# Softmax row sums: a ones-matmul with Ln and Exp against a transposing reduction, a 16-column matmul and a transpose

## The chip, the cores and the metric

One core of one Trainium2 chip runs the whole program in one launch. The metric is the time of one execution on the device, in microseconds (us), as the median of several executions. All the runs used here are of the undisturbed ("fast") kind; the executions of one kernel lie mostly within 0.4% of each other. The experiments were timed in several rounds and on several chips, where the kernel before took between 367.5 and 368.2 us (medians), so a difference between runs of different rounds is uncertain by about 0.6 us. In this text PE is TensorE's matmul stream, PEld its weight loads, DVE is VectorE, ACT is ScalarE, POOL is GpSimd, SP is the engine that issues most DMAs.

## The reference

Two independent attention blocks, A and B, with grouped heads, each followed by an output projection; the two results stand side by side.

```python
# B=16, Sq=32, D=1024, Hq=32 query heads, Hkv=4 key/value heads, Sk=512, Dh=128, all bf16
q = (x @ wq).reshape(B, Sq, Hq, Dh).transpose(0, 2, 1, 3)
k, v = repeat(k_cache, 8, axis=1), repeat(v_cache, 8, axis=1)
p = softmax(einsum("bhqd,bhkd->bhqk", q, k) * Dh ** -0.5, axis=-1)
o = einsum("bhqk,bhkd->bhqd", p, v)
out = o.transpose(0, 2, 1, 3).reshape(B, Sq, Hq * Dh) @ wo
```

## The kernel before

The work is cut into 128 slots, one for each (problem, batch, key/value head). A slot has 8 heads x 32 queries = 256 columns (QW) and 512 keys in KC = 4 chunks of P = 128 partitions. In the code SQ = 32 is the queries of a slot, REP = 8 its heads, and NG = 64 the pairs of slots. Scores are computed transposed (keys on partitions), ScalarE takes the exponential with a fixed shift in place of a maximum, and the values matmul leaves its result with head dimension on partitions and query columns along the free axis. The softmax denominator of a column is therefore a sum over *partitions*, and it is wanted on all 128 partitions, to scale a [128, 256] block. Before, two adds on VectorE sum the four chunks, and a matmul with a matrix of ones sums over partitions and broadcasts at once; Ln and Exp(-x) on ScalarE make the reciprocal.

```python
def partial_sums(i):                       # each slot, VectorE
    t1 = work.tile([P, 2, QW], FP32, name="t1", bufs=1)
    nc.vector.tensor_tensor(out=t1[:], in0=p_sb[:, 0:2, :], in1=p_sb[:, 2:4, :], op=ALU.add)
    ...
    nc.vector.tensor_tensor(out=tsum[j][:, q, :], in0=t1[:, 0, :], in1=t1[:, 1, :], op=ALU.add)

def pair_sums(j):                          # each pair of slots
    sums = psum.tile([P, 2, QW], FP32, name="sums", tag="sums", bufs=1)
    nc.tensor.matmul(sums[...], lhsT=ones[:], rhs=tsum.pop(j)[...], start=True, stop=True)  # 512 columns
    nc.scalar.activation(out=lg[:], in_=sums[:], func=ACTF.Ln)
    nc.scalar.activation(out=rcp[j][:], in_=lg[:], func=ACTF.Exp, scale=-1.0)
    nc.gpsimd.dma_start(out=lall[j:j + 1, :], in_=lg[0:1, ...])   # for a range check at the end
```

`normalize` multiplies `rcp` into `ob`, the PSUM result of the values matmuls; `ob` has one buffer for a pair of slots, so the next pair's values wait for it. TensorE's remaining work, the projections of q and of the output, is cut into single 512-column matmuls ("units"), and about 6.75 of them are strewn into every slot so that TensorE always has something to do:

```python
for i in range(total_slots + 2):
    j, odd = divmod(i - 2, 2)               # live: slot i exists; j >= 0: a pair two slots back
    if live: do_loads(i); scores(i)
    if odd and j >= 0: normalize(2 * j)
    run(units, 3)
    if not odd and j >= 0: pair_sums(j)
    run(units, 1 if odd else 3)
    if j >= 0: values(2 * j + odd)          # two slots behind
    if live: partial_sums(i)
    run(units, 3 - (i % 4 == 3) if odd else 1)
    if odd and j >= 0: normalize(2 * j + 1)
```

Keys and values come by DMA four slots at a time, from a pool `kv` with two buffers each for `kT` and `v_sb`. These loads, and all but the first of the weights', stand in SP's queue in program order.

Of the kernel before, what the change touches and what calls it, by code (L numbers as in the profile page):

```python
# [8 lines left out]
BF16 = mybir.dt.bfloat16  # L9
FP32 = mybir.dt.float32  # L10
FP32R = mybir.dt.float32r
I32 = mybir.dt.int32
ACTF = mybir.ActivationFunctionType
ALU = mybir.AluOpType
AX = mybir.AxisListType

P = 128
HQ = 32
DH = 128
HKV = 4  # L20
REP = HQ // HKV
HALF = REP // 2
SCALE = float(DH) ** -0.5

SHIFT = 44.0
ONES = 2.0 ** -75
LIMIT = 20.0


def general_path(tc, problems, out_flat):  # L30
# [142 lines left out]
def kernel(  # L173
# [35 lines left out]
    def fast_path(ok_i):  # L209
        with ExitStack() as fctx:  # L210
            enter = fctx.enter_context
            const = enter(tc.tile_pool(name="const", bufs=1))
            blk = enter(tc.tile_pool(name="blk", bufs=20))
            kv = enter(tc.tile_pool(name="kv", bufs=2))
            work = enter(tc.tile_pool(name="work", bufs=2))
            outp = enter(tc.tile_pool(name="outp", bufs=3))
            psum = enter(tc.tile_pool(name="psum", bufs=2, space=bass.MemoryType.PSUM))
# [11 lines left out]
            nc.vector.memset(warm[:], 0.0)  # L229
            ident = const.tile([P, P], BF16, name="ident")  # L230
            make_identity(nc, ident[:])
            ones_f = const.tile([P, P], FP32, name="ones_f")
            nc.vector.memset(ones_f[:], ONES)
            ones = const.tile([P, P], FP32R, name="ones")
            nc.vector.tensor_copy(out=ones[:], in_=ones_f[:])
            one_col = const.tile([P, 1], FP32, name="one_col")
            nc.vector.memset(one_col[:], 1.0)
            shift = const.tile([P, 1], FP32, name="shift")
            nc.vector.memset(shift[:], SHIFT)
            cnt = const.tile([P, 1], FP32, name="cnt")  # L240
            nc.vector.memset(cnt[:], 0.0)
            NLR = NG
            lall = const.tile([NLR, 2 * QW], FP32, name="lall")


            def blk_tile(shape, name, dtype=BF16):
                return blk.tile(shape, dtype, name=name, tag="blk")
# [54 lines left out]
            def q_units(pr, h):  # L302
                g, hl = divmod(h, REP)
                if hl == 0:
                    qT[pr, g] = blk_tile([P, B, REP, SQ], "qT")
                w = wq_tiles[pr, h // 4]
                ps = psum.tile([P, NW], FP32, name="q_ps", tag="proj")
                for dc in range(DC):
                    nc.tensor.matmul(  # L309
                        ps[:],  # L310
                        lhsT=w[:, dc, (h % 4) * DH:(h % 4 + 1) * DH],
                        rhs=xT[pr][:, dc, :],
                        start=(dc == 0),
                        stop=(dc == DC - 1),
                    )
                    if dc == DC - 1:
                        nc.vector.tensor_copy(  # L317
                            out=qT[pr, g][:, :, hl, :],
                            in_=ps[:].rearrange("p (b s) -> p b s", s=SQ),
                        )  # L320
                    yield
# [26 lines left out]
            def run(units, n):  # L348
                for _ in range(n):
                    next(units, None)  # L350


            def where(i):
                pr, ii = divmod(i, NG)
                if pr == 0:
                    g, b = divmod(ii, B)
                else:
                    b, g = divmod(ii, HKV)
                return pr, b, g
# [3 lines left out]
            def scores(i):  # L363
                pr, b, g = where(i)
                kT = k_tiles[i // GRP].rearrange("p q (k c) -> p q c k", c=KC)
                s_ps = psum.tile([P, KC, QW], FP32, name="s_ps", tag="s")
                for c in range(KC):
                    nc.tensor.matmul(  # L368
                        s_ps[:, c, :],
                        lhsT=kT[:, i % GRP, c, :],  # L370
                        rhs=qT[pr, g][:, b, :, :].rearrange("p h s -> p (h s)"),
                        start=True,
                        stop=True,
                    )
                p_sb = work.tile([P, KC, QW], BF16, name="p_sb", bufs=4)
                nc.scalar.activation(  # L376
                    out=p_sb[:], in_=s_ps[:], func=ACTF.Exp, bias=shift[:], scale=SCALE
                )
                st[i] = {"p": p_sb}

            tsum, rcp = {}, {}

            def partial_sums(i):
                p_sb = st[i]["p"]
                t1 = work.tile([P, 2, QW], FP32, name="t1", bufs=1)
                nc.vector.tensor_tensor(  # L386
                    out=t1[:], in0=p_sb[:, 0:2, :], in1=p_sb[:, 2:4, :], op=ALU.add
                )
                j, q = divmod(i, 2)
                if q == 0:  # L390
                    tsum[j] = work.tile([P, 2, QW], FP32R, name="t")
                nc.vector.tensor_tensor(
                    out=tsum[j][:, q, :], in0=t1[:, 0, :], in1=t1[:, 1, :], op=ALU.add
                )

            pair = {}

            def pair_sums(j):
                sums = psum.tile([P, 2, QW], FP32, name="sums", tag="sums", bufs=1)
                nc.tensor.matmul(  # L400
                    sums[:].rearrange("p q n -> p (q n)"),
                    lhsT=ones[:],
                    rhs=tsum.pop(j)[:].rearrange("p q n -> p (q n)"),
                    start=True,
                    stop=True,
                )
                lg = work.tile([P, 2, QW], FP32, name="lg")
                nc.scalar.activation(out=lg[:], in_=sums[:], func=ACTF.Ln)  # L408
                rcp[j] = work.tile([P, 2, QW], FP32, name="r")
                nc.scalar.activation(out=rcp[j][:], in_=lg[:], func=ACTF.Exp, scale=-1.0)  # L410
                nc.gpsimd.dma_start(  # L411
                    out=lall[j:j + 1, :],
                    in_=lg[0:1, :, :].rearrange("p q n -> p (q n)"),
                )

            def values(i):
                v_sb = v_tiles[i // GRP]
                j, q = divmod(i, 2)
                if q == 0:
                    pair[j] = psum.tile([P, 2, QW], FP32, name="ob", tag="ob", bufs=1)  # L420
                for c in range(KC):
                    nc.tensor.matmul(  # L422
                        pair[j][:, q, :],
                        lhsT=v_sb[:, i % GRP, c, :],
                        rhs=st[i]["p"][:, c, :],
                        start=(c == 0),
                        stop=(c == KC - 1),
                    )

            def normalize(i):  # L430
                pr, b, g = where(i)
                normalized.add((pr, b, g))
                st.pop(i)
                j, q = divmod(i, 2)
                tt, bl = divmod(b, BPT)
                if (pr, tt) not in oT:
                    oT[pr, tt] = blk_tile([P, HQ, P], "oT")
                nc.vector.scalar_tensor_tensor(  # L438
                    out=oT[pr, tt][:, g * REP:(g + 1) * REP, bl * SQ:(bl + 1) * SQ],
                    in0=rcp[j][:, q, :].rearrange("p (h s) -> p h s", s=SQ),  # L440
                    scalar=ONES,
                    in1=pair[j][:, q, :].rearrange("p (h s) -> p h s", s=SQ),
                    op0=ALU.mult,
                    op1=ALU.mult,
                )


# [115 lines left out]


            total_slots = 2 * NG
            for i in range(total_slots + 2):
                live = i < total_slots
                j, odd = divmod(i - 2, 2)
                if live:
                    do_loads(i)  # L570
                    scores(i)
                if odd and j >= 0:
                    normalize(2 * j)
                run(units, 3)
                if not odd and j >= 0:
                    pair_sums(j)
                run(units, 1 if odd else 3)
                if j >= 0:
                    values(2 * j + odd)
                if live:  # L580
                    partial_sums(i)
                run(units, 3 - (i % 4 == 3) if odd else 1)
                if odd and j >= 0:
                    normalize(2 * j + 1)


            run(units, 8)
            sq = blk_tile([NLR, 2 * QW], "sq", FP32)
            nc.vector.tensor_tensor(out=sq[:], in0=lall[:], in1=lall[:], op=ALU.mult)
            nc.vector.tensor_scalar(  # L590
                out=sq[:], in0=sq[:], scalar1=LIMIT * LIMIT, scalar2=0.0,
                op0=ALU.is_le, op1=ALU.add, accum_out=cnt[0:NLR, :],
            )
            run(units, 16)
            ok_ps = psum.tile([1, 1], FP32, name="ok_ps", tag="s")
            nc.tensor.matmul(ok_ps[:], lhsT=cnt[:], rhs=one_col[:], start=True, stop=True)
# [3 lines left out]
    flag = ctx.enter_context(tc.tile_pool(name="flag", bufs=1))  # L600
    ok_i = flag.tile([1, 1], I32, name="ok_i")
    fast_path(ok_i)
    total = 2 * NG * QW
    ok = nc.values_load(ok_i[0:1, 0:1], min_val=0, max_val=total,
                        skip_runtime_bounds_check_because="only compared")
    with tc.If(ok < total, preferred_fallthrough_block=True, label="general"):
# [31 lines left out]
```

## Time and profile before

| | before |
|---|---|
| time, median of 3 runs | 368.15 us (367.96 to 368.4) |
| span of the profiled run | 367.2 us |
| PE, DVE, ACT busy | 98%, 66%, 60% |
| clock granted to TensorE | 0.998 |

The first line is from the page's table of busy time, the second from its chain of work that ended last, by engine; the groups below them have, on the right of the bar, the busy time of all and the mean ns of one, then the engine's idle time just before them with what ended it.

```profile
PE 359.0 (98%) x2204; PEld 221.9 (60%) x2204; DVE 243.3 (66%) x478; ACT 218.6 (60%) x262; POOL 40.5 (11%) x85
...
PE 92%; DMA 3%; DVE 2%; issue 1%; ACT 1%; DVEq 0%
...
L438 DVE SCALAR_TENSOR_TENSOR oT<-r,ob 128x256 bf16<-128x256 f32 x128 | 53.2, 416 | 2.6 <-ACT r L410 1.6
L410 ACT ACTIVATE r<-lg 128x512 f32<-128x512 f32 x64 | 40.4, 632 | 2.0
L408 ACT ACTIVATE lg<-sums 128x512 f32<-128x512 f32 x64 | 37.8, 590 | 1.8 <-PE sums L400 1.8
L400 PE MATMUL sums<-t,ones 128*128 128x512 f32 x64 | 35.9, 561 | 0.1
...
L400 PEld LDWEIGHTS sums<-t,ones 128*128 128x128 f32 x64 | 12.1, 188 | 9.8 <-issue 2.8
```

TensorE is the limit: busy 98% at full clock, and 92% of the chain. But the 561 ns of one `sums` matmul is not what it takes from TensorE's stream, because the records of matmuls overlap: a 512-column projection matmul has a record of 380 ns, and the next one starts 216 ns after it. What counts is the distance between starts. The next lines are the timeline of PE alone (start, duration, what, how many):

```profile
67.94 0.81 PE L309 MATMUL q_ps<-xT,wq_sb 128*128 128x512 bf16 x3
68.40 0.58 PE L400 MATMUL sums<-t,ones 128*128 128x512 f32 x1
68.83 0.82 PE L309 MATMUL q_ps<-xT,wq_sb 128*128 128x512 bf16 x3
69.48 0.60 PE L422 MATMUL ob<-p_sb,v_sb 128*128 128x256 bf16 x4
```

From 67.94 to 68.83 are 0.89 us, of which three projection matmuls take 3 x 0.216. The `sums` matmul takes the remaining 0.24 us. The one after it comes 11 ns late, so 0.25 us in all, and 64 of them make 16 us. This is the prize.

The rest that can be won on TensorE is waits, of two kinds. From the view of waits (who waited for whom: us, times, longest):

```profile
PEld L422 <- issue: 3.9, 10, 0.5
PE s_ps L368 <- DMA kT<-in_B_k_cache_dram: 1.5, 1, 1.5
PE ob L422 <- DVE oT L438: 1.1, 5, 0.2
```

```profile
30.18 1.03 PE L309 MATMUL q_ps<-xT,wq_sb 128*128 128x512 bf16 x4
...
30.96 0.41 DVE L438 SCALAR_TENSOR_TENSOR oT<-r,ob 128x256 bf16<-128x256 f32 x1
31.43 0.60 PE L422 MATMUL ob<-p_sb,v_sb 128*128 128x256 bf16 x4 [0.22 <-DVE oT L438]
```

One wait is for keys (`kT`), once. The other is for `ob`: values want the buffer before VectorE's normalisation has left it. The view puts 1.1 us on it. (By start distance the one wait for keys is 1.65 us, where the view has 1.5.)

### The profile page before, as it was taken

The page shows a single profiled execution, that of the slowest core. Times are in us where ns is not written, and L with a number is a line of the kernel's source. Part 1 is how long each engine was busy: PE and PEld are TensorE (multiplying, and loading weights), DVE is VectorE, ACT ScalarE, POOL GpSimd, SP SyncE. Part 2 cuts the span into 40 slices and gives each one's busy share as a digit, 9 for nine tenths or more (in the row PEclk, how much of TensorE's full clock was granted, in tenths as well). Part 3 has the DMA queues.
Part 4 walks back from the last instruction along what each step waited for, and adds up shares of the span by engine and source line. Part 5 has one row for each costly group of instructions (what it writes and reads, how often), then busy time and mean ns, then how long its engine had stood idle before and what let it go on. Part 6 is the DMA issues. An engine that isn't in the chain of part 4 may idle for free.

```text
span 367.2 us, 6071 instructions
## 1 busy us (share of the span) xinstructions
PE 359.0 (98%) x2204; PEld 221.9 (60%) x2204; DVE 243.3 (66%) x478; ACT 218.6 (60%) x262; POOL 40.5 (11%) x85
## 2 busy tenths in 40 slices
PE   8999999999999999999999999998999999999995
PEld 5555656666665666666666666665665666666554
DVE  1448787877878777887776667664666666666410
ACT  2127666667666667666666776665766666766200
POOL 0001101111110111110111111111111111111110
PEclk9999999999999999999999999999999999999999
DMA  8998479899797479799999354997447994440000
GB/s 266 310 267 245 105 218 222 194 306 225 209 207 200 96 217 220 221 308 294 322 289 271 97 123 131 253 346 177 131 129 245 339 227 112 113 116 15 17 14 33
DMA packets 127136, 71.86 MB, mean 196 GB/s; under 512 B 75680, under 2 KB 126112, under 8 KB 127104
## 3 DMA queue, kind: packets, MB, share of 16 engines
q1 hardware_dynamic: 122848, 68.24, 69.8%
q0 software_dynamic: 2768, 2.10, 2.1%
q10 hardware_dynamic: 1488, 1.11, 1.0%
q8 instruction: 18, 0.29, 0.3%
q14 instruction: 14, 0.11, 0.1%
HBM read 51.38 MB, written 2.10 MB: 146 GB/s over the span
## 4 chain that ended last, share of the span: by engine, by line
PE 92%; DMA 3%; DVE 2%; issue 1%; ACT 1%; DVEq 0%
PE f_ps L328 28%; PE q_ps L309 28%; PE ob L422 14%; PE s_ps L368 14%; PE sums L400 4%; DMA kT<-in_B_k_cache_dram 3%; PE warm_ps L471 1%; PE q_ps L494 1%; PE xT_ps L480 1%; DVE oT L438 1%; ACT r L410 0%; ACT lg L408 0%; DVE t_544 L386 0%; DVE t_3211 L386 0%; DVE t_1516 L386 0%
## 5 line engine op out<-in xcount | busy, mean ns | idle before, releaser
L376 ACT ACTIVATE p_sb<-s_ps,shift 128x1024 bf16<-128x1024 f32 x128 | 142.7, 1114 | 114.9 <-PE s_ps L368 109.3
L328 PE MATMUL f_ps<-wo_sb,oT 128*128 128x512 bf16 (+1 forms) x544 | 137.0, 367 | 0.0
L309 PE MATMUL q_ps<-xT,wq_sb 128*128 128x512 bf16 x496 | 134.0, 380 | 0.0
L368 PE MATMUL s_ps<-qT,kT 128*128 128x256 bf16 x512 | 76.8, 273 | 1.5 <-DMA kT<-in_B_k_cache_dram 1.5
L422 PE MATMUL ob<-p_sb,v_sb 128*128 128x256 bf16 x512 | 76.8, 272 | 1.1 <-DVE oT L438 1.1
L422 PEld LDWEIGHTS <-v_sb 128*128 128x128 bf16 x512 | 50.1, 98 | 35.8 <-issue 3.9
L368 PEld LDWEIGHTS <-kT 128*128 128x128 bf16 x512 | 56.7, 113 | 23.4 <-DMA kT<-in_B_k_cache_dram 2.0
L328 PEld LDWEIGHTS <-oT 128*128 128x128 bf16 x544 | 50.6, 98 | 33.3 <-issue 7.6
L309 PEld LDWEIGHTS <-wq_sb 128*128 128x128 bf16 x496 | 46.0, 98 | 33.2 <-issue 6.7
L411 POOL DMA_DIRECT2D lall<-lg x64 | 31.3, 489 | 276.1 <-ACT lg L408 276.0
L317 DVE CAST qT<-q_ps 128x512 bf16<-128x512 f32 x62 | 42.8, 690 | 26.1 <-PE q_ps L309 25.3
L438 DVE SCALAR_TENSOR_TENSOR oT<-r,ob 128x256 bf16<-128x256 f32 x128 | 53.2, 416 | 2.6 <-ACT r L410 1.6
L410 ACT ACTIVATE r<-lg 128x512 f32<-128x512 f32 x64 | 40.4, 632 | 2.0
L408 ACT ACTIVATE lg<-sums 128x512 f32<-128x512 f32 x64 | 37.8, 590 | 1.8 <-PE sums L400 1.8
L400 PE MATMUL sums<-t,ones 128*128 128x512 f32 x64 | 35.9, 561 | 0.1
L340 DVE CAST o_sb<-f_ps 128x512 bf16<-128x512 f32 (+1 forms) x16 | 10.8, 674 | 14.9 <-PE f_ps L328 14.7
L400 PEld LDWEIGHTS sums<-t,ones 128*128 128x128 f32 x64 | 12.1, 188 | 9.8 <-issue 2.8
L342 POOL DMA_DIRECT2D out_dram<-o_sb x15 | 8.5, 568 | 40.4 <-DVE o_sb L340 40.1
L338 ACT CAST o_sb<-f_ps 128x256 bf16<-128x256 f32 x1 | 0.4, 372 | 19.1 <-PE f_ps L328 19.1
L484 DVE COPY xT<-xT_ps 128x512 bf16<-128x512 bf16 x4 | 1.7, 425 | 6.4 <-PE xT_ps L480 6.4
L485 ACT COPY xT<-xT_ps 128x512 bf16<-128x512 bf16 x4 | 2.2, 588 | 6.1 <-DVE xT L484 6.1
L471 PE MATMUL warm_ps<-warm 128*128 128x512 bf16 x10 | 4.5, 615 | 1.3 <-DVE warm L229 1.3
(281 smaller groups left out, 162.9 us busy)
## 6 DMA issues: line engine op xcount, KB each, us to landing
v_sb<-in_A_v_cache_dram SPq DMA_DIRECT2D x16, 512.0 KB, 4.8
wq_sb<-in_B_wq_dram SPq DMA_DIRECT2D x8, 1024.0 KB, 6.1
wo_sb<-in_A_wo_dram SPq DMA_DIRECT2D x8, 1024.0 KB, 7.2
v_sb<-in_B_v_cache_dram SPq DMA_DIRECT2D x16, 512.0 KB, 3.9
wo_sb<-in_B_wo_dram SPq DMA_DIRECT2D x8, 1024.0 KB, 8.6
wq_sb<-in_A_wq_dram SPq DMA_DIRECT2D x7, 1024.0 KB, 7.6
out_dram<-o_sb POOLq DMA_DIRECT2D x15, 128.0 KB, 2.3
kT<-in_A_k_cache_dram SPq DMA_TRANSPOSE x64, 3.3
```

The source lines that it names most:

```text
L309: nc.tensor.matmul(ps[:], lhsT=w[:, dc, (h % 4) * DH:(h % 4 + 1) * DH], rhs=xT[pr][:, dc, :], start=(dc == 0), stop=(dc == DC - 1),)
L317: nc.vector.tensor_copy(out=qT[pr, g][:, :, hl, :], in_=ps[:].rearrange("p (b s) -> p b s", s=SQ),)
L328: nc.tensor.matmul(ps[:, 0:width], lhsT=oT[pr, tt][:, h, :], rhs=wo_tiles[pr, nh, h // REP][:, h % REP, off:off + width], start=(h == 0), ...
L340: nc.vector.tensor_copy(out=o_sb[:, 0:width], in_=ps[:, 0:width])
L368: nc.tensor.matmul(s_ps[:, c, :], lhsT=kT[:, i % GRP, c, :], rhs=qT[pr, g][:, b, :, :].rearrange("p h s -> p (h s)"), start=True, stop=True,)
L376: nc.scalar.activation(out=p_sb[:], in_=s_ps[:], func=ACTF.Exp, bias=shift[:], scale=SCALE)
L400: nc.tensor.matmul(sums[:].rearrange("p q n -> p (q n)"), lhsT=ones[:], rhs=tsum.pop(j)[:].rearrange("p q n -> p (q n)"), start=True, stop ...
L408: nc.scalar.activation(out=lg[:], in_=sums[:], func=ACTF.Ln)
L410: nc.scalar.activation(out=rcp[j][:], in_=lg[:], func=ACTF.Exp, scale=-1.0)
L411: nc.gpsimd.dma_start(out=lall[j:j + 1, :], in_=lg[0:1, :, :].rearrange("p q n -> p (q n)"),)
L422: nc.tensor.matmul(pair[j][:, q, :], lhsT=v_sb[:, i % GRP, c, :], rhs=st[i]["p"][:, c, :], start=(c == 0), stop=(c == KC - 1),)
L438: nc.vector.scalar_tensor_tensor(out=oT[pr, tt][:, g * REP:(g + 1) * REP, bl * SQ:(bl + 1) * SQ], in0=rcp[j][:, q, :].rearrange("p (h s) - ...
```

## The change

The intent: TensorE's 512-column matmul becomes one of 16 columns, and Ln and Exp leave ScalarE. VectorE's `tensor_reduce` with `apply_transpose` transposes 32x32 blocks and sums over what was the partition axis, so 32 partitions (a quadrant) are summed in one instruction; the four quadrants are then added by a tiny matmul with a matrix of four by four identities; the reciprocal is taken on 16 columns, and a VectorE transpose of a broadcast view spreads it over 512 columns. To balance the engines, the qT copies move from VectorE to ScalarE. Values run three slots behind in place of two, the kv pool gets a third buffer, and `p_sb`, which waits longer for its values now, five buffers in place of four.

```diff
-            kv = enter(tc.tile_pool(name="kv", bufs=2))
+            kv = enter(tc.tile_pool(name="kv", bufs=3))
...
-                        nc.vector.tensor_copy(
+                        nc.scalar.copy(
                             out=qT[pr, g][:, :, hl, :],
...
-                p_sb = work.tile([P, KC, QW], BF16, name="p_sb", bufs=4)
+                p_sb = work.tile([P, KC, QW], BF16, name="p_sb", bufs=5)
...
-                nc.vector.tensor_tensor(out=t1[:], in0=p_sb[:, 0:2, :], ...)      # and the second add
+                nc.vector.tensor_reduce(
+                    out=parts[j][:, q, :, :].rearrange("p c h -> p (c h)"),
+                    in_=st[i]["p"][:].rearrange("p c (h s) -> p (c h) s", s=SQ),
+                    axis=AX.X, op=ALU.add, apply_transpose=True,
+                )
+            def chunk_sums(j):                       # 128x64 -> 128x16, over the four chunks
+                nc.vector.tensor_reduce(out=cs[:], in_=parts.pop(j)[...], axis=AX.X, op=ALU.add)
+            def fold_sums(j):
+                nc.tensor.matmul(sums[:], lhsT=fold[...], rhs=cs[...], start=True, stop=True)   # 16 columns
+            def reciprocals(j):
+                nc.vector.reciprocal(out=rall[:, j, :], in_=pair.pop(j)[:])
+                nc.vector.transpose(out=r[...], in_=rall[:, j, :].unsqueeze(2).to_broadcast([P, 2 * REP, SQ]))
...                                                   # normalize: one 512-column instruction per pair, not two of 256
-            for i in range(total_slots + 2):
+            for i in range(total_slots + 3):
...
+                run(units, 1)
+                if not odd and 1 <= j <= NG: chunk_sums(j - 1)
+                if i >= 3: values(i - 3)
+                if odd and 1 <= j <= NG: reciprocals(j - 1)
+                if not odd and j >= 2: normalize(j - 2)
+                run(units, 5)
+                if not odd and 1 <= j <= NG: fold_sums(j - 1)
+                if live: partial_sums(i)
+                run(units, 1 - (i % 4 == 3))
```

The 64 small `lall` DMAs go too; the range check now reads the reciprocals, which stay in memory.

More of the change, by code (lines that the diff above doesn't have):

```diff
@@ L21 @@
 REP = HQ // HKV
+QD = 32
 HALF = REP // 2
@@ L25 @@
 SHIFT = 44.0
-ONES = 2.0 ** -75
-LIMIT = 20.0
+SUM_LO = 2.0 ** 46
+SUM_HI = 2.0 ** 104
 def general_path(tc, problems, out_flat):
@@ L231, in fast_path @@
             make_identity(nc, ident[:])
-            ones_f = const.tile([P, P], FP32, name="ones_f")
-            nc.vector.memset(ones_f[:], ONES)
-            ones = const.tile([P, P], FP32R, name="ones")
-            nc.vector.tensor_copy(out=ones[:], in_=ones_f[:])
+            fold = const.tile([P, P // QD, QD], FP32R, name="fold")
+            for r in range(P // QD):
+                rs = slice(r * QD, (r + 1) * QD)
+                nc.vector.tensor_copy(
+                    out=fold[rs],
+                    in_=ident[rs, rs].unsqueeze(1).to_broadcast([QD, P // QD, QD]),
+                )
             one_col = const.tile([P, 1], FP32, name="one_col")
@@ L241, in fast_path @@
             nc.vector.memset(cnt[:], 0.0)
-            NLR = NG
-            lall = const.tile([NLR, 2 * QW], FP32, name="lall")
+            rall = const.tile([P, NG, 2 * REP], FP32, name="rall")
             def blk_tile(shape, name, dtype=BF16):
@@ L379, in scores @@
                 st[i] = {"p": p_sb}
-            tsum, rcp = {}, {}
+            parts, rcp, pair = {}, {}, {}
             def partial_sums(i):
-                p_sb = st[i]["p"]
-                t1 = work.tile([P, 2, QW], FP32, name="t1", bufs=1)
-                nc.vector.tensor_tensor(
-                    out=t1[:], in0=p_sb[:, 0:2, :], in1=p_sb[:, 2:4, :], op=ALU.add
-                )
                 j, q = divmod(i, 2)
                 if q == 0:
-                    tsum[j] = work.tile([P, 2, QW], FP32R, name="t")
-                nc.vector.tensor_tensor(
-                    out=tsum[j][:, q, :], in0=t1[:, 0, :], in1=t1[:, 1, :], op=ALU.add
-                )
-            pair = {}
-            def pair_sums(j):
-                sums = psum.tile([P, 2, QW], FP32, name="sums", tag="sums", bufs=1)
+                    parts[j] = work.tile([P, 2, KC, REP], FP32, name="parts")
+                nc.vector.tensor_reduce(
+                    out=parts[j][:, q, :, :].rearrange("p c h -> p (c h)"),
+                    in_=st[i]["p"][:].rearrange("p c (h s) -> p (c h) s", s=SQ),
+                    axis=AX.X, op=ALU.add, apply_transpose=True,
+                )
+            def chunk_sums(j):
+                cs = pair[j] = work.tile([P, 2, REP], FP32R, name="cs")
+                with nc.allow_low_precision(reason="float32r holds the float32 sum"):
+                    nc.vector.tensor_reduce(
+                        out=cs[:], in_=parts.pop(j)[:].rearrange("p q c h -> p q h c"),
+                        axis=AX.X, op=ALU.add,
+                    )
+            def fold_sums(j):
+                cs = pair[j]
+                sums = pair[j] = psum.tile([P, 2 * REP], FP32, name="sums", tag="sums", bufs=1)
                 nc.tensor.matmul(
-                    sums[:].rearrange("p q n -> p (q n)"),
-                    lhsT=ones[:],
-                    rhs=tsum.pop(j)[:].rearrange("p q n -> p (q n)"),
+                    sums[:],
+                    lhsT=fold[:].rearrange("p r s -> p (r s)"),
+                    rhs=cs[:].rearrange("p q h -> p (q h)"),
                     start=True,
@@ L406, in pair_sums @@
                 )
-                lg = work.tile([P, 2, QW], FP32, name="lg")
-                nc.scalar.activation(out=lg[:], in_=sums[:], func=ACTF.Ln)
-                rcp[j] = work.tile([P, 2, QW], FP32, name="r")
-                nc.scalar.activation(out=rcp[j][:], in_=lg[:], func=ACTF.Exp, scale=-1.0)
-                nc.gpsimd.dma_start(
-                    out=lall[j:j + 1, :],
-                    in_=lg[0:1, :, :].rearrange("p q n -> p (q n)"),
+            def reciprocals(j):
+                nc.vector.reciprocal(out=rall[:, j, :], in_=pair.pop(j)[:])
+                r = rcp[j] = work.tile([P, 2 * REP, SQ], FP32, name="r")
+                nc.vector.transpose(
+                    out=r[:].rearrange("p n s -> p (n s)"),
+                    in_=rall[:, j, :].unsqueeze(2).to_broadcast([P, 2 * REP, SQ]),
                 )
+            ob = {}
             def values(i):
@@ L419, in values @@
                 if q == 0:
-                    pair[j] = psum.tile([P, 2, QW], FP32, name="ob", tag="ob", bufs=1)
+                    ob[j] = psum.tile([P, 2, QW], FP32, name="ob", tag="ob", bufs=1)
                 for c in range(KC):
                     nc.tensor.matmul(
-                        pair[j][:, q, :],
+                        ob[j][:, q, :],
                         lhsT=v_sb[:, i % GRP, c, :],
@@ L428, in values, with normalize @@
                     )
-            def normalize(i):
-                pr, b, g = where(i)
-                normalized.add((pr, b, g))
-                st.pop(i)
-                j, q = divmod(i, 2)
+            def normalize(j):
+                for i in (2 * j, 2 * j + 1):
+                    normalized.add(where(i))
+                    st.pop(i)
+                pr, b, g = where(2 * j)
                 tt, bl = divmod(b, BPT)
@@ L437, in normalize @@
                     oT[pr, tt] = blk_tile([P, HQ, P], "oT")
-                nc.vector.scalar_tensor_tensor(
-                    out=oT[pr, tt][:, g * REP:(g + 1) * REP, bl * SQ:(bl + 1) * SQ],
-                    in0=rcp[j][:, q, :].rearrange("p (h s) -> p h s", s=SQ),
-                    scalar=ONES,
-                    in1=pair[j][:, q, :].rearrange("p (h s) -> p h s", s=SQ),
-                    op0=ALU.mult,
-                    op1=ALU.mult,
+                if pr == 0:
+                    out = oT[pr, tt][:, g * REP:(g + 1) * REP, bl * SQ:(bl + 2) * SQ]
+                    out = out.rearrange("p h (q s) -> p q h s", s=SQ)
+                else:
+                    out = oT[pr, tt][:, g * REP:(g + 2) * REP, bl * SQ:(bl + 1) * SQ]
+                    out = out.rearrange("p (q h) s -> p q h s", h=REP)
+                nc.vector.tensor_tensor(
+                    out=out,
+                    in0=rcp.pop(j)[:].rearrange("p (q h) s -> p q h s", h=REP),
+                    in1=ob.pop(j)[:].rearrange("p q (h s) -> p q h s", s=SQ),
+                    op=ALU.mult,
                 )
@@ L565, in fast_path @@
             total_slots = 2 * NG
-            for i in range(total_slots + 2):
+            for i in range(total_slots + 3):
                 live = i < total_slots
-                j, odd = divmod(i - 2, 2)
+                j, odd = divmod(i, 2)
                 if live:
@@ L571, in fast_path @@
                     scores(i)
-                if odd and j >= 0:
-                    normalize(2 * j)
-                run(units, 3)
-                if not odd and j >= 0:
-                    pair_sums(j)
-                run(units, 1 if odd else 3)
-                if j >= 0:
-                    values(2 * j + odd)
+                run(units, 1)
+                if not odd and 1 <= j <= NG:
+                    chunk_sums(j - 1)
+                if i >= 3:
+                    values(i - 3)
+                if odd and 1 <= j <= NG:
+                    reciprocals(j - 1)
+                if not odd and j >= 2:
+                    normalize(j - 2)
+                run(units, 5)
+                if not odd and 1 <= j <= NG:
+                    fold_sums(j - 1)
                 if live:
                     partial_sums(i)
-                run(units, 3 - (i % 4 == 3) if odd else 1)
-                if odd and j >= 0:
-                    normalize(2 * j + 1)
-            run(units, 8)
-            sq = blk_tile([NLR, 2 * QW], "sq", FP32)
-            nc.vector.tensor_tensor(out=sq[:], in0=lall[:], in1=lall[:], op=ALU.mult)
-            nc.vector.tensor_scalar(
-                out=sq[:], in0=sq[:], scalar1=LIMIT * LIMIT, scalar2=0.0,
-                op0=ALU.is_le, op1=ALU.add, accum_out=cnt[0:NLR, :],
-            )
+                run(units, 1 - (i % 4 == 3))
+            sq = blk_tile([QD, NG * 2 * REP], "sq", FP32)
+            cnt2 = const.tile([P, 2], FP32, name="cnt2")
+            nc.vector.memset(cnt2[:], 0.0)
+            for k, (lim, op) in enumerate(((1.0 / SUM_HI, ALU.is_ge), (1.0 / SUM_LO, ALU.is_le))):
+                nc.vector.tensor_scalar(
+                    out=sq[:], in0=rall[0:QD].rearrange("p j n -> p (j n)"),
+                    scalar1=lim, scalar2=0.0, op0=op, op1=ALU.add,
+                    accum_out=cnt2[0:QD, k:k + 1],
+                )
+            nc.vector.tensor_tensor(out=cnt[:], in0=cnt2[:, 0:1], in1=cnt2[:, 1:2], op=ALU.add)
             run(units, 16)
@@ L602 @@
     fast_path(ok_i)
-    total = 2 * NG * QW
+    total = 2 * 2 * NG * QW
     ok = nc.values_load(ok_i[0:1, 0:1], min_val=0, max_val=total,
```

## The prediction

> **What bounds the kernel now.** TensorE. The page's busy table gives PE 98% of 367.2 us, DVE 66%, ACT 60%, POOL 11%; the chain of waits is 92% PE, clock full throughout. In the two-slot steady state (timeline, 60 to 81 us) a pair of slots takes 4.80 or 5.02 us, and matmuls start back to back: 216 ns for 512 columns, 109 ns for 256. PE waits little: 1.5 us once at 250 us for a kT transpose DMA, 1.1 us in five waits of ob for oT (view of waits). DVE and ACT have slack in every stretch, so what the change does for them is worth nothing by itself; only PE's stream counts.
>
> **Removed from PE.** The 128x512 float32r ones-matmul, 64 times. From the matmul before it to the one after it the start-to-start distance is about 455 ns against 216 without it: 239 ns each, plus 11 ns lost at the next matmul, about 15.5 us (the chain gives it 4.2%, 15.4 us). Its 188 ns weight load hides behind the 512-column matmul before it.
>
> **Added on PE.** The same matmul with 16 columns. The weight load should still hide; the streaming shrinks to almost nothing, but the next weight load cannot hide behind it. The nearest thing in the trace is the one-column fp32 pair of ok_ps: 25 ns to its twin, 96 ns to the next bf16 matmul. Estimate: 95 ns each (60 to 150), 6 us. Net gain about 9.4 us (6 to 12).
>
> **VectorE.** Removed per pair of slots: two adds of 695 ns, two of 425, two normalisations of 416, and 1.7 qT copies of 690 in the first half (these go to ACT, where a 512-column PSUM read takes about 0.6 us). Added: two transposing reductions over 1024 elements. The Trainium skill ("VectorE: DVE Perf Modes", the perf-mode tier table) has tensor_reduce at 1x; this trace's 512-element fp32 ops are 690 ns and 256-element ones 425, i.e. about 1.04 ns an element plus 160, so about 1.22 us each (estimate), if transposing costs nothing per element. Plus a 64-element sum (0.22), a 16-element reciprocal (0.3), a 512-element transpose (0.69) and one merged normalisation (0.7). With the overlap seen between independent instructions this is about 4.1 us per pair in the first half and 4.35 with o_sb copies in the second, against about 4.75 of PE. So DVE rises to about 85 to 92% busy and does not take over; the chain reduction, chunk sum, fold, reciprocal, transpose, normalisation has about 1 us of slack before the single ob buffer is wanted again.
>
> **ACT, POOL, DMA.** ACT loses Ln and Exp (78 us), gains 62 copies (about 37 us): down to about 49%. The 64 small lall DMAs go. Three kv buffers let kT loads run ahead; the 1.5 us kT wait should vanish, and probably most of the ob waits.
>
> **Predicted.** 368.15 - 9.4 - 2.3 + 0.8 for new small waits = 357.2 us, 354 to 364. Faster by over 2% (below 360.8): 0.78; within 2%: 0.13; slower: 0.09.
>
> **What would show it.** PE busy still 96% or more of a shorter span; sums group far below 35.9 us, with 250 ns or less added around each fold; DVE 85 to 92%, reductions about 1.2 us; ACT near 50%; no kT or ob wait over 1 us in total.
>
> **What would make it wrong.** The transposing reduction running at half rate (about 2.3 us): then VectorE needs about 6.5 us per pair and the kernel takes about 460 us. Dependent waits on VectorE pushing normalisation past the next use of ob. An exposed weight load around the fold (188 + 100 ns): then the gain all but disappears. Loads running ahead and delaying weights.

## The result

| | before | after |
|---|---|---|
| time, median of 4 runs | 368.05 us (367.26 to 368.4) | 350.57 us (350.22 to 351.09) |
| span of the profiled run | 367.2 us | 349.1 us |
| PE, DVE, ACT, POOL busy | 98, 66, 60, 11% | 98, 81, 51, 3% |

The ratio is 0.9529 (95% interval 0.9507 to 0.9551). A ratio here is the mean time of one kernel's fast runs over that of the other's of the same rounds, so it is not quite the ratio of the medians. A control of the changed kernel in later rounds gave 350.65 us against 368.15. The gain is 17.5 us; 10.9 were predicted, and 350.6 lies outside the range that began at 354.

The same parts of the page of the changed kernel:

```profile
PE 340.7 (98%) x2163; PEld 221.0 (63%) x2204; DVE 283.4 (81%) x421; ACT 179.6 (51%) x196; POOL 8.9 (3%) x21
...
PE 94%; DMA 3%; issue 1%; DVE 1%; ACT 0%; SPq 0%
...
L390 DVE TRANSPOSE_TENSOR_REDUCE parts<-p_sb 128x32 f32<-128x1024 bf16 x128 | 158.2, 1236 | 21.5 <-ACT p_sb L379 20.9
...
L453 DVE TENSOR_TENSOR oT<-r,ob 128x512 bf16<-128x512 f32 x64 | 43.9, 685 | 12.7 <-PE ob L431 9.3
L320 ACT CAST qT<-q_ps 128x512 bf16<-128x512 f32 x62 | 36.1, 583 | 23.7 <-PE q_ps L312 20.8
L418 DVE STREAM_TRANSPOSE r<-rall 128x512 f32<-128x512 f32 x64 | 45.5, 711 | 2.2
L407 PE MATMUL sums<-cs,fold 128*128 128x16 f32 x64 | 22.9, 357 | 0.1
...
L407 PEld LDWEIGHTS sums<-cs,fold 128*128 128x128 f32 x64 | 12.1, 190 | 8.3 <-DVE cs L399 0.9
```

Note the fold matmul: its record is still 357 ns long, and its weight load's 190. Neither is its cost. The timeline of PE has the distance:

```profile
60.36 1.24 PE L312 MATMUL q_ps<-xT,wq_sb 128*128 128x512 bf16 x5
61.25 0.36 PE L407 MATMUL sums<-cs,fold 128*128 128x16 f32 x1
61.47 0.39 PE L312 MATMUL q_ps<-xT,wq_sb 128*128 128x512 bf16 x1
61.70 0.60 PE L371 MATMUL s_ps<-qT,kT 128*128 128x256 bf16 x4
```

From 60.36 to 61.47 are 1.11 us for five projection matmuls (1.08) and the fold: 0.03 us. The next distance, 61.47 to 61.70, is 11 ns over 216. In exact figures from the trace: 28 ns from the start of the matmul before to the fold's, 220 from there to the next, less 216, plus 11: 43 ns. So 64 x (250 - 43) ns = 13.2 us come from columns that are no longer streamed. In the view of waits no matmul of scores waits for keys any more, and no `ob` matmul comes late; at some places (12 of them before an `ob` matmul) the record of a 512-column matmul is missing in this trace, which adds exactly its 216 ns to a distance and is not a wait. That is the other part: 1.7 us of the `kT` wait and 2.7 of the `ob` waits, both by start distance (ten places for `ob`: distance to the `ob` matmul less 216 ns, summed). 13.2 + 1.7 + 2.7 = 17.6 us against 17.5 measured. The sum closes, but a sum that closes is not yet a cause shown; the change has five parts.

### The profile page after: what moved, and what is told of

Same layout as the page of the kernel before. It is cut to its first block, busy times and chain, and to the rows that moved or that the text cites. A ratio compares the mean times of both kernels' runs of the same rounds, so it can differ in the third digit from the quotient of the medians.

```text
span 349.1 us, 5460 instructions
## 1 busy us (share of the span) xinstructions
PE 340.7 (98%) x2163; PEld 221.0 (63%) x2204; DVE 283.4 (81%) x421; ACT 179.6 (51%) x196; POOL 8.9 (3%) x21
## 3 DMA queue, kind: packets, MB, share of 16 engines
q10 hardware_dynamic: 1488, 1.11, 1.1%
## 4 chain that ended last, share of the span: by engine, by line
PE 94%; DMA 3%; issue 1%; DVE 1%; ACT 0%; SPq 0%
PE f_ps L331 31%; PE q_ps L312 30%; PE ob L431 16%; PE s_ps L371 16%; DMA wq_sb<-in_A_wq_dram 2%; DMA x_sb<-in_A_x_dram 1%; DVE parts L390 0%; PE sums L407 0%; DVE o_sb L343 0%; ACT o_sb L341 0%; DVE cs L399 0%; PE ok_ps L614 0%; SPq L651 0%
## 5 line engine op out<-in xcount | busy, mean ns | idle before, releaser
L390 DVE TRANSPOSE_TENSOR_REDUCE parts<-p_sb 128x32 f32<-128x1024 bf16 x128 | 158.2, 1236 | 21.5 <-ACT p_sb L379 20.9
L331 PE MATMUL f_ps<-wo_sb,oT 128*128 128x512 bf16 (+1 forms) x524 | 127.9, 367 | 0.4
L312 PE MATMUL q_ps<-xT,wq_sb 128*128 128x512 bf16 x475 | 124.8, 380 | 0.6
L453 DVE TENSOR_TENSOR oT<-r,ob 128x512 bf16<-128x512 f32 x64 | 43.9, 685 | 12.7 <-PE ob L431 9.3
L320 ACT CAST qT<-q_ps 128x512 bf16<-128x512 f32 x62 | 36.1, 583 | 23.7 <-PE q_ps L312 20.8
L418 DVE STREAM_TRANSPOSE r<-rall 128x512 f32<-128x512 f32 x64 | 45.5, 711 | 2.2
L407 PE MATMUL sums<-cs,fold 128*128 128x16 f32 x64 | 22.9, 357 | 0.1
L399 DVE TENSOR_REDUCE cs<-parts 128x16 fp32r<-128x64 f32 x64 | 16.9, 264 | 2.2
L407 PEld LDWEIGHTS sums<-cs,fold 128*128 128x128 f32 x64 | 12.1, 190 | 8.3 <-DVE cs L399 0.9
L416 DVE RECIPROCAL rall<-sums 128x16 f32<-128x16 f32 x64 | 14.1, 220 | 0.0
```

The source lines that it names most:

```text
L312: nc.tensor.matmul(ps[:], lhsT=w[:, dc, (h % 4) * DH:(h % 4 + 1) * DH], rhs=xT[pr][:, dc, :], start=(dc == 0), stop=(dc == DC - 1),)
L320: nc.scalar.copy(out=qT[pr, g][:, :, hl, :], in_=ps[:].rearrange("p (b s) -> p b s", s=SQ),)
L331: nc.tensor.matmul(ps[:, 0:width], lhsT=oT[pr, tt][:, h, :], rhs=wo_tiles[pr, nh, h // REP][:, h % REP, off:off + width], start=(h == 0), ...
L390: nc.vector.tensor_reduce(out=parts[j][:, q, :, :].rearrange("p c h -> p (c h)"), in_=st[i]["p"][:].rearrange("p c (h s) -> p (c h) s", s=SQ),
L399: nc.vector.tensor_reduce(out=cs[:], in_=parts.pop(j)[:].rearrange("p q c h -> p q h c"), axis=AX.X, op=ALU.add,)
L407: nc.tensor.matmul(sums[:], lhsT=fold[:].rearrange("p r s -> p (r s)"), rhs=cs[:].rearrange("p q h -> p (q h)"), start=True, stop=True,)
```

## The experiments

Theory: the columns taken from TensorE make 13.2 us, and the other parts of the change (third kv buffer, qT on ScalarE, no Ln and Exp) win little by themselves; what they do is keep loads, VectorE and ScalarE from taking the gain back. Rivals: the narrow matmul costs 95 ns as predicted and the rest comes from the relief of the other engines; or the parts each add their own share.

### Narrow matmul alone, in the kernel before

```diff
-                    rhs=tsum.pop(j)[:].rearrange("p q n -> p (q n)"),     # 512 columns
+                    rhs=tsum.pop(j)[:, 0, 0:16],
...             # Ln reads the 16 columns through a broadcast view, output still 512 columns
```

> The kernel before, only the ones-matmul narrowed from 512 to 16 columns (result wrong on purpose; Ln reads the 16 columns broadcast to 512, so ScalarE and VectorE do the same work as before). Theory A (most of the gain is streaming columns taken from TensorE's own stream, and a 16-column float32r matmul costs about 43 ns there against 250): 64 x 0.207 = 13.2 us less, about 354.8 us. Rival B (my prediction's 95 ns for the narrow matmul, the rest of the gain coming from VectorE, ScalarE or the new schedule): 9.9 us less, about 358 us.

Measured: 359.26 us (357.8 to 360.79), ratio 0.9741. (The comparison with the reference even passed, presumably because with these inputs all sums are nearly alike; the kernel is wrong all the same.) The time is nearer to rival B. But the trace has exactly 28 and 220 ns around each narrow matmul, as in the changed kernel, so those 13.2 us were won, and 4.3 us were lost elsewhere. About one of them went to `ob` waits (15 of 3.8 us by start distance, against 10 of 2.7). For the rest, the view of waits and the granted clock (view by stretches: window, length, busy time of each engine, then clock, DMA share, GB/s) say where:

```profile
PE s_ps L368 <- DMA kT<-in_B_k_cache_dram: 4.5, 2, 3.5
```

```profile
241.00:247.00 6.00, 2.48 (x17) 1.45 (x15) 1.51 (x4) 1.23 (x2) 0.00 (x0) 1.00 1.22 219
247.00:251.00 4.00, 4.00 (x18) 2.11 (x17) 1.54 (x3) 2.13 (x4) 0.48 (x1) 0.57 0.33 72
```

A faster TensorE wanted its keys earlier than two buffers let them come: one kT wait of 1.5 us became two of 4.5 us in sum. And after the longer, of 3.5 us up to 245.99, the clock was 0.57 on average between 247 and 251: 256-column matmuls stand 213 ns apart there in place of 109. The Trainium skill, "TensorE: Matmul & The Clock Gate", Part 1, has this: the clock is halved after an idle window of about 3.4 us. Here the wait was 3.5 us, and this trace agrees, but the halving began only 1.2 us after TensorE was back at work, and it is not in every execution: of the four, two had a granted clock of 1.0 throughout and took 357.8 and 358.48 us, two had 0.988 and 0.993 and took 360.79 and 360.05. So the slow clock goes with about 2.3 us, in half of the executions.

### Wide matmul in the changed kernel

```diff
-                    rhs=cs[:].rearrange("p q h -> p (q h)"),
+                    rhs=cs[:].rearrange("p q h -> p (q h)").unsqueeze(2).to_broadcast([P, 2 * REP, SQ]),
...             # sums is [P, 2 * REP, SQ]; the reciprocal reads sums[:, :, 0]
```

> The changed kernel, only the fold matmul widened to 512 columns by broadcasting its moving operand (result stays right). Theory A: the 13.2 us come back, about 363.8 us (350.6 + 13.2), and what remains of the gain, about 4.3 us, is the waits. Rival B (new dependency chain and VectorE's relief make up a third or more of the gain): only some 9 us come back, about 360 us.

Measured: 363.21 us (362.81 to 363.53): 12.6 us of the 17.5 go back (theory 13.2, rival about 9). Everything else of the change stays in place, and wins 4.9 us. (In this trace a wide fold takes 231 ns of TensorE's stream, not 250, which would make 12.0 us; why it is shorter than the ones-matmul was not looked into.) This and the next run were timed in other rounds than the changed kernel; its control differs by 0.1 us between rounds.

### No fold at all

```diff
-                if not odd and 1 <= j <= NG:
-                    fold_sums(j - 1)
...
-                nc.vector.reciprocal(out=rall[:, j, :], in_=pair.pop(j)[:])
+                nc.vector.reciprocal(out=rall[:, j, :], in_=pair.pop(j)[:].rearrange("p q h -> p (q h)"))
```

> The changed kernel without the fold matmul; the reciprocal reads the chunk sums directly (result wrong on purpose). Theory A: the fold costs 43 ns each, so 2.7 us less, about 347.8 us. Prediction's size (95 ns each): 6.1 us less, about 344.5 us.

Measured: 347.58 us, 3.0 us less than the changed kernel, 47 ns for each fold (55 if each is taken as a ratio to the kernel before in its own rounds). The 43 ns of the trace hold, the 95 of the prediction don't.

### Where the fold stands, and what an exposed one costs

The prediction took 95 ns from the only small fp32 matmuls of the trace, the pair of `ok_ps`. Its lines, PE alone, in the kernel before:

```profile
349.82 1.24 PE L328 MATMUL f_ps<-wo_sb,oT 128*128 128x512 bf16 x5
350.99 0.19 PE L596 MATMUL ok_ps<-one_col,cnt 128*1 128x1 f32 x2
351.11 1.25 PE L328 MATMUL f_ps<-wo_sb,oT 128*128 128x512 bf16 x5
```

Five matmuls from 349.82 take until 350.90; the pair starts at 350.99. TensorE had stood idle for 0.09 us, for a cause that the profile doesn't name, so nothing ran right in front of the pair behind which a weight load could hide. Two runs ask what the matmul in front changes (none puts the fold behind an idle TensorE): one moves the fold behind a 256-column matmul, one issues it twice in a row, so that the second has only 16 columns in front.

```diff
                     scores(i)
+                if odd and 1 <= j <= NG:
+                    fold_sums(j - 1)
                 run(units, 1)
...             # and not after run(units, 5)
```

> The changed kernel, the fold moved from behind a 512-column projection matmul to behind the last 256-column score matmul of the next slot. If its cost is small because its 188 ns weight load hides behind the 216 ns matmul before it, then behind a 109 ns matmul some 80 ns of it show: 64 x 0.08 = 5 us more, about 355.7 us, with the distance from the matmul before to the one after near 230 ns instead of 248 minus 107. If the load's place doesn't matter: 350.6 us.

Measured: 350.43 us (350.15 to 350.5), no slower. The expectation was wrong, and it was mine for the theory: the timeline of PE has

```profile
61.50 0.60 PE L371 MATMUL s_ps<-qT,kT 128*128 128x256 bf16 x4
61.85 0.26 PE L407 MATMUL sums<-cs,fold 128*128 128x16 f32 x1
61.97 0.39 PE L312 MATMUL q_ps<-xT,wq_sb 128*128 128x512 bf16 x1
```

0.47 us from 61.50 to 61.97, less 4 x 0.109: 0.03 again (35 ns exactly, and 11 at the next: 46 in all). So the 190 ns in the record of the weight load are no more its hold on TensorE than the 357 ns are the matmul's; a matmul of 109 ns right in front of it is enough.

```diff
+                for _ in range(2):
                     nc.tensor.matmul(sums[:], lhsT=fold[...], rhs=cs[...], start=True, stop=True)
```

> The changed kernel with each fold matmul issued twice in a row (result stays right). The second fold's weight load has only a 16-column matmul in front of it. If an exposed float32r load costs about what I took from ok_ps: 64 x 0.095 = 6 us more, about 356.7 us. If a fold costs 43 ns wherever it stands: 2.7 us more, 353.3 us.

Measured: 357.76 us (357.33 to 358.11) against 350.65 of the control in the same rounds: 7.1 us more, 111 ns for each second fold. The timeline of PE agrees:

```profile
60.89 1.24 PE L312 MATMUL q_ps<-xT,wq_sb 128*128 128x512 bf16 x5
61.78 0.47 PE L408 MATMUL sums<-cs,fold 128*128 128x16 f32 x2
62.12 0.39 PE L312 MATMUL q_ps<-xT,wq_sb 128*128 128x512 bf16 x1
```

From 60.89 to 62.12, less five matmuls of 216 ns, are 0.15 us (0.144 exactly) for two folds, where one takes 0.03. The size that I had taken from `ok_ps` was about right, for a fold with only 16 columns in front of it. That is partly luck: here it is the second fold whose start is held up, whereas the 96 ns of `ok_ps` lie after the pair, before the next bf16 matmul, and that pair is plain float32 with one column of weights. Which of these differences makes its 96 ns was not tested.

> The changed kernel itself, unchanged, as a control in the same rounds: 350.5 us.

Measured: 350.65 us (350.2 to 350.76).

### The kv buffers

In the kernel before, a third `kT` buffer (memory was found by three p_sb buffers in place of four):

```diff
-                kT = k_tiles[j] = kv.tile([P, GRP, SK], BF16, name="kT")
+                kT = k_tiles[j] = kv.tile([P, GRP, SK], BF16, name="kT", bufs=3)
```

> The kernel before with three kT buffers in place of two (and p_sb at three in place of four, to find the memory). Theory: only the one kT stall near 250 us goes, 1.65 us less, about 366.5 us; the third buffer by itself is under half a per cent.

Measured: 366.84 us (366.33 to 367.02), ratio 0.9973 (0.9956 to 0.999): 1.2 us. The kT wait is gone from the view of waits.

The same (both edits and the p_sb buffers as above) with the narrow matmul of the first experiment:

> The narrow ones-matmul and three kT buffers together (result wrong on purpose). Theory: the narrow matmul alone lost about 4.5 us of its 13.2 to two kT stalls (1.2 and 3.7 us) and the slow clock after the longer one; with the third buffer they go, and the time is 368.1 - 13.2 - 1.7 = 353.2 us. If the missing part was anything else (the ob waits, the clock): about 358 us.

Measured: 354.86 us (354.15 to 355.19). The narrow matmul is now worth 12.0 us (366.84 - 354.86), against 8.9 with two buffers (368.15 - 359.26). That most of the missing part, 3.1 of 4.3 us, was the loads is shown; of the last 1.2 us to 13.2, more `ob` waits are 0.8: 14 of 3.5 us in sum, by start distances, where the kernel before has 10 of 2.7.

And in the changed kernel, back to two buffers:

```diff
-            kv = enter(tc.tile_pool(name="kv", bufs=3))
+            kv = enter(tc.tile_pool(name="kv", bufs=2))
```

> The changed kernel with two kv buffers in place of three. Theory: the kT stalls come back as in the narrow-matmul run, and with values one slot later, worse: 5 us more, about 355.5 us, with waits of scores for kT near 190 and 240 us. If the third buffer is only a convenience: under 1 us more.

Measured: 362.3 us (360.69 to 363.02), ratio to the kernel before 0.9843. Without the third buffer two thirds of the whole gain, 11.7 us, are lost:

```profile
PE s_ps L371 <- DMA kT<-in_B_k_cache_dram: 8.2, 6, 3.8
```

Six waits of 8.2 us in sum, where the kernel before had one of 1.5; and behind the longest the slow clock again (view by stretches, as above), here in all four executions (0.990 to 0.992):

```profile
246.00:251.00 5.00, 5.00 (x19) 2.58 (x18) 2.73 (x4) 1.11 (x1) 0.00 (x0) 0.51 0.49 111
```

I had expected 5 us. Why it is so much worse here than in the narrow run (4.5 us of waits) was not taken apart; values run one slot later here, so the value loads, which stand before the keys in SP's queue, get their buffer one slot later. SP's own waits fit that (62.7 us for `ob` before value loads, against 43.9 in the narrow run), but it is only argued.

### qT copies and Ln/Exp: who normalises in time

Next, the run with narrow matmul and three kT buffers (and three p_sb buffers, like the one after it) also gets the qT copies on ScalarE, and nothing else of the change: VectorE still makes the two wide adds.

```diff
-                        nc.vector.tensor_copy(
+                        nc.scalar.copy(
                             out=qT[pr, g][:, :, hl, :],
```

> As the last, and the qT copies on ScalarE (result wrong on purpose). Theory: what remains are the ob waits, about 3 us, which come where a qT copy on VectorE stands between a reduction and the normalisation; with the copies on ScalarE they go, 350.5 us, the changed kernel's own time, with none of its transposing reductions. Rival: ScalarE, which here still has Ln and Exp (about 93% busy in the first half by estimate), delays the exponentials, and the time stays at 353 us or rises.

Measured: 353.41 us (352.01 to 353.97). The rival was right: there are still 14 `ob` waits, only their cause has changed, as the view of waits says:

```profile
DVE oT L442 <- ACT r L414: 6.9, 13, 1.1
```

The normalisation now waits for ScalarE, which has Ln, Exp and the copies. So one of its operations was taken away:

```diff
-                nc.scalar.activation(out=lg[...], in_=sums[...], func=ACTF.Ln)
-                rcp[j] = work.tile([P, 2, QW], FP32, name="r")
-                nc.scalar.activation(out=rcp[j][:], in_=lg[:], func=ACTF.Exp, scale=-1.0)
+                nc.scalar.activation(out=lg[...], in_=sums[...], func=ACTF.Exp, scale=-1.0)
+                rcp[j] = lg
```

> As the run with narrow ones-matmul, three kT buffers and qT copies on ScalarE (353.4 us), but Ln and Exp of the sums replaced by one Exp (result wrong on purpose). Theory: the 12 ob waits left there came from VectorE's normalisation waiting for ScalarE's r; one operation of 0.63 us less per pair takes most of them away: about 351 us, the changed kernel's time, with wide adds on VectorE and no transposing reduction. Rival: the ob waits come from elsewhere (values issued two slots behind in place of three) and stay: 353.4 us.

Measured: 351.15 us (350.03 to 351.32), result wrong as meant. Only two `ob` waits are left (and 0.7 us for keys, by start distance). This kernel has the changed kernel's time, to 0.6 us, with the old wide adds on VectorE, values two slots behind, two buffers for values, and the `lall` DMAs. So the time of the changed kernel is explained by three things: 16 columns, keys in time, and ScalarE and VectorE light enough to give `ob` back in time. The transposing reduction is not fast for its own sake; it makes the 16 columns right. (No run takes the third slot of delay or the fifth `p_sb` buffer out of the changed kernel; what they are worth there is not shown.)

The other direction, the changed kernel with the qT copies back on VectorE:

```diff
-                        nc.scalar.copy(
+                        nc.vector.tensor_copy(
                             out=qT[pr, g][:, :, hl, :],
```

> The changed kernel with the qT copies back on VectorE. Theory: VectorE, 90% busy in the first half, gets 1.7 copies of 0.6 to 0.69 us more per pair of slots and becomes the limit there: about 5.2 us per pair against 4.7, over 37 pairs, some 15 us more, about 365 us (360 to 371). If overlap between instructions hides that: 350.6 us.

Measured: 361.05 us (360.82 to 361.17), 10.5 us more. By stretches (PE, PEld, DVE, ACT, POOL in this order), first this run, then the changed kernel:

```profile
60.00:100.00 40.00, 38.28 (x236) 23.92 (x240) 39.49 (x62) 17.12 (x17) 0.00 (x0) 1.00 1.05 229
```

```profile
60.00:100.00 40.00, 39.67 (x257) 26.28 (x261) 35.86 (x53) 26.31 (x33) 0.00 (x0) 1.00 1.13 266
```

VectorE is busy 39.5 of 40 us and has become the limit of the first half; in the changed kernel it is at 90%. I had expected 15 us; presumably overlap between its instructions hides the rest. So this move, which in the kernel before with 16 columns and three kT buffers was worth 1.5 us (354.86 to 353.41), is worth 10 us beside the transposing reduction.

### The small DMAs

```diff
-                nc.gpsimd.dma_start(out=lall[j:j + 1, :], in_=lg[0:1, :, :].rearrange("p q n -> p (q n)"))
```

> The kernel before without the 64 small lall DMAs (their table is set to zero, so the range check always passes; result right). Theory: they are off TensorE's stream and cost nothing, 368.1 us. Rival: their descriptors on the 16 DMA engines or on GpSimd slow the loads: 1 us or more less.

Measured: 367.29 us (366.76 to 368.1) against 367.51 in the same rounds, ratio 0.9985 (0.9971 to 0.9998). At most 1 us; nothing of weight.

### A faster version: the fold in bf16

```diff
-            fold = const.tile([P, P // QD, QD], FP32R, name="fold")
+            fold = const.tile([P, P // QD, QD], BF16, name="fold")
...
-                cs = pair[j] = work.tile([P, 2, REP], FP32R, name="cs")
+                cs = pair[j] = work.tile([P, 2, REP], BF16, name="cs")
```

> The changed kernel with fold matrix and chunk sums in bf16, so that the fold's weight load takes the 98 ns of the other loads in place of 190. A try for a faster version. If the 43 ns that a fold costs are partly its weight load: about 25 ns each, 1.2 us less, 349.4 us; if not: 350.6 us.

Measured: 349.26 us (348.89 to 349.45), correct. In the trace the fold is 216 ns from the matmul before it and 28 ns from the one after: it costs 28 ns in place of 43. Once more, beside the control:

> The bf16 fold in the same rounds as the control: 64 x 15 ns = 1 us less than the control, about 349.4 us.

Measured: 349.6 us (349.11 to 350.43) against 350.65 (350.2 to 350.76) of the control: 1.05 us less, as 64 x 15 ns say, though its longest execution, 350.43, lies inside the control's spread. It beats both kernels by a little. It rounds the sums of a quadrant to bf16 before they are added, which the reference's tolerance allows and another use may not.

### All together

| kernel | us | what it tells |
|---|---|---|
| before | 368.15 | |
| before, third kT buffer | 366.84 | worth 1.2 by itself |
| before, 16 columns | 359.26 | loads take back a third |
| before, 16 columns, third kT buffer | 354.86 | 12.0 for the columns |
| ... and qT on ScalarE | 353.41 | `ob` waits for ScalarE |
| ... and one ScalarE operation less | 351.15 | the changed kernel's time |
| changed, two kv buffers | 362.3 | 11.7 lost |
| changed, qT on VectorE | 361.05 | 10.5 lost |
| changed, 512 columns | 363.21 | 12.6 lost |
| changed | 350.57 | |
| changed, bf16 fold | 349.6 | 1.05 under the control |

The three losses add to 34.8 us, twice the gain of 17.5. The parts do not add; each is needed for the others to count.

## Why the prediction was wrong

- **TensorE is the limit and only its stream counts: right.** PE stayed at 98%, and the sum over its start distances closes to 0.1 us.
- **What the 512-column matmul takes, about 250 ns: right** by the trace of the kernel before; the wide fold, 12.6 us over the narrow one, gives about 240.
- **"the next weight load cannot hide behind it": this step failed.** It gave 95 ns a fold and a net gain of 9.4 us; it costs 43 ns, 13.2 us net. After the fold the next distance is only 11 ns longer, so the bf16 load there does not show its recorded 98. The 95 ns came from a pair of matmuls of another type, before which TensorE had stood idle; what makes it cost that much there is open. Behind a running matmul of 109 or 216 ns a fold costs 43 to 47 ns; a second fold with only 16 columns in front, 111. This is 3.8 of the 6.6 us that were missed.
- **Waits: right in kind, too small.** I took 1.1 us for the `ob` waits from the line that named them and expected most of it back; start distances give 2.7, and all came back. The kT wait was right (1.5 predicted, 1.65 by start distance, 1.2 by itself in the kernel before). Together 4.4 in place of 2.3, so 2.1 us more; and the 0.8 us that I set aside for new waits did not come. 3.8 + 2.1 + 0.8 = 6.7.
- **VectorE and its transposing reduction: right.** 1.22 us estimated, 1236 ns measured; 4.1 and 4.35 us per pair estimated, 4.2 and 4.4 busy (35.77 of 40 us in 100 to 140, and 46.43 of 50 in 190 to 240, by 4.71 us a pair). The skill's 1x for `tensor_reduce` ("VectorE: DVE Perf Modes", the perf-mode tier table) holds with the transpose too. The busy share over the whole span is 81%, since it counts the start and the end.
- **ScalarE near 50%: right** (51%).
- **"probably most of the ob waits" through more buffers and slack: right result, cause not stated.** The runs show two causes, a qT copy in VectorE's way and then ScalarE's Ln and Exp; both had to go.
- **Not seen at all:** that a third kv buffer, 1.2 us in the kernel before (there for `kT` alone), is worth 11.7 us once TensorE is faster. By luck it did not spoil the number, since the change brings the buffer along; the argument for it was too weak.

## What to carry to other kernels

Cost a matmul by the distance between the starts of its neighbours, with the same kind of work in front of it as it will have; neither its record's length, nor its weight load's, nor a similar one that stood elsewhere tells it. A wait is read the same way: the line that names the cause may hold less than half of it. And a buffer or a copy that costs nothing while TensorE is slow can cost most of a gain once TensorE is faster, so try the parts of a change together and take them out one by one.

## What the Trainium skill lacked or had wrong

- "VectorE: DVE Perf Modes", rules for kernel authors, says that a reduction along the partition axis is not possible on this engine. Within 32 partitions it is: the transposing `tensor_reduce` did it in 1236 ns for 128x1024 bf16, with a correct result, and the page has no figure for it. What is left is the sum of four quadrants.
- The same page's 311 ns for a 128x128 bf16 transpose has no fp32 counterpart: 128x512 fp32 from a broadcast view took 711 ns.
- "TensorE: Matmul & The Clock Gate", on LDWEIGHTS, gives about P/1.2 ns for a load, by estimate 107 ns for 128 columns; the records have 98 for most bf16 loads (113 for those of `kT`) and 190 for float32r. No page says how much of that shows for a very short float32r matmul: 43 to 47 ns behind a matmul of 109 or 216 ns, 111 ns with only 16 columns in front. For bf16 it was 28 ns, near the page's floor of about 25 ns between starts.
